# Attention and a two-layer product on one core: norm products on GpSimd, the first batch transposed on TensorE, out matmuls ahead of the scores, w_out in column halves

## The chip, the cores and the metric

The kernel runs on one core of a Trainium2 chip. The metric is the device time of one execution in microseconds (us). Of the timed runs five were classed slow (four of the kernel before in the later series, one of the experiment without the lead); they count in the medians quoted, but in no ratio, and where a slow run moves a difference the text says so. TensorE is called PE in the profile, its weight loads PEld, VectorE DVE, ScalarE ACT, GpSimd POOL and SyncE SP. A line number such as L178 is a line of the kernel that was profiled, so the same statement has different numbers in different kernels.

## The reference

Eight batches, twelve heads, 448 tokens, 64 numbers per head. The result of the attention, heads side by side, goes through a product with w_in (768 x 2048), an activation with a sine, and a product with w_out (2048 x 768).

```python
def rmsnorm(x, g):
    return x / np.sqrt(np.mean(x * x, axis=-1, keepdims=True) + 1e-06) * g
q_n, k_n = rmsnorm(q, g_q), rmsnorm(k, g_k)
scores = np.matmul(q_n, k_n.transpose(0, 1, 3, 2)) / np.sqrt(64)
attn = softmax(scores)                       # over the last axis
x = heads_side_by_side(np.matmul(attn, v))   # (3584, 768)
h = x @ w_in
g = h + np.sin(alpha * h) ** 2 / (alpha + 1e-09)
out = g @ w_out
```

## The kernel before

For each batch there are two stages. An *attention stage* takes six pairs of heads: scores, exponentials, and the product with v. Between them, as "fillers", stand the steps of the out product (w_out) of the batch before, and, as "background", the norm tasks of the batch to come. A *first product stage* is the product with w_in and the sine part ("snake"). Odd batches have 48 filler steps in their attention stage and are called short below; even ones from 2 on have 64 and are called long. A *chunk* is q and k of two pairs of heads; a batch has three chunks. The norm of a chunk, as a list of tasks of which the schedule takes a few per pair:

```python
def square(w): nc.gpsimd.tensor_mul(st[w], qk[ci][:, w], qk[ci][:, w])     # ScalarE for the first chunks
def fold_g():  nc.gpsimd.tensor_mul(qk[ci][:, 1], qk[ci][:, 1], gg)        # VectorE for the first chunks
def reduce(w): nc.vector.reduce_sum(st["ms"][:, w, :], st[w], axis=AX.X)
def rsqrt():   # ScalarE: Ln, then Exp
def scale(w):  nc.vector.tensor_mul(n, x, inv)    # two or three pieces per w, bf16 out
def transpose(): nc.sync.dma_start_transpose(...) # two per chunk
return [lambda: (square(0), square(1)), fold_g, none, lambda: reduce(0), lambda: reduce(1), none,
        rsqrt, lambda: (scale(0), scale(1), transpose())]
```

The schedule of an attention stage (cut):

```python
for p in range(NP):
    scores(pi, 0); scores(pi, 1)
    if p: attend(pi - 1)      # product with v; reciprocal on ScalarE; xT on VectorE
    scores(pi, 3)
    bg(per_slot)
    fill(part[2])             # half of the pair's out steps
    bg(per_slot)
    scores(pi, 2)
    fill(part[3] - part[2])
    bg(per_slot)
    fill(part[4] - part[3])
    bg(per_slot)
...
attend(last pair)
first_product(b)
```

PSUM has four tiles of two banks each for scores, products with v and both products. A tile is free again when its last reader, often VectorE, is done.

The softmax here doesn't subtract the row's maximum and nothing guards it: scores larger than these inputs give would overflow.

## Time and profile before

| | before |
|---|---|
| time, median | 544.5 us |
| span of the profiled run | 543.7 us |
| PE / DVE / ACT / POOL busy | 84% / 54% / 64% / 38% |
| first score matmul | 34.65 us |
| attention stage, short / long | 42.0 / 43.4 us (batches 3 and 4) |
| first product, matmuls | 18.3 us |

The stages in this table run from the end of the matmuls of the first product to the start of the next batch's, so the 3 us of transition belong to the attention stage; the prediction's windows put them into the first product. This is what TensorE waited for in the kernel before, in the view of waits. The columns are the waiting line, what it waited for, us in total, how many times, and the longest:

```profile
PE sc L215 <- DMA qkT<-qkn: 34.6, 1, 34.6
PE ops L305 <- DVE g_sb L258: 11.4, 6, 1.9
PE sc L215 <- DVE xT L244: 10.9, 6, 2.8
```

One wait of 34.6 us for the first transposes, six waits for the last snake piece at the transitions, six for xT in the stages. What the list does not show is the time that matmuls took longer at a lower clock.

### The profile page before, as it was taken

Reading aid. Unit: us, or ns where it says so; the run is one execution under the profiler, and the core shown is the slowest. Engines: PE = TensorE matmul, PEld = TensorE weight load, DVE = VectorE, ACT = ScalarE, POOL = GpSimd, SP = SyncE. Lnnn points to the kernel's source line nnn. Section 1 sums busy time; section 2 is a strip of 40 time slices with the busy share of each in tenths; the row PEclk is TensorE's granted clock in tenths of the full one; section 3 lists DMA queues with packets and bytes.
Section 4 is the critical chain, followed back from the end, with each engine's and each line's share of the span. In section 5 each row is a group of like instructions: output and inputs, shape, how many; then the busy total and the mean of one; then the engine's idle time right before and its main releaser. Section 6 shows DMA issues by size and latency. Waiting matters only on the chain.

```text
span 543.7 us, 7414 instructions
## 1 busy us (share of the span) xinstructions
PE 458.2 (84%) x2816; PEld 214.7 (39%) x2816; DVE 293.5 (54%) x379; ACT 346.0 (64%) x550; POOL 206.2 (38%) x167
## 2 busy tenths in 40 slices
PE   0035589797989999897989999897989999899996
PEld 0011235343444445343444445343444445344553
DVE  0628745368555774377555774377556765222531
ACT  2226377686786657775686657775687658876810
POOL 3004924834257313734258304734257404100400
PEclk9996589799999999898998999898999999999998
DMA  9993599935815565535715564545715551011013
GB/s 226 202 196 76 136 161 210 159 60 125 208 10 72 133 149 113 52 69 128 196 10 72 131 160 103 51 78 119 198 11 70 132 100 27 1 43 45 2 32 85
DMA packets 86276, 56.40 MB, mean 104 GB/s; under 512 B 67552, under 2 KB 81888, under 8 KB 86240
## 3 DMA queue, kind: packets, MB, share of 16 engines
q1 hardware_dynamic: 63344, 42.29, 34.9%
q0 software_dynamic: 21808, 11.80, 17.5%
q10 hardware_dynamic: 1088, 1.84, 1.0%
q8 instruction: 22, 0.36, 0.3%
q14 instruction: 14, 0.11, 0.1%
HBM read 45.69 MB, written 11.01 MB: 104 GB/s over the span
## 4 chain that ended last, share of the span: by engine, by line
PE 63%; DMA 14%; DVE 12%; issue 4%; ACT 3%; POOL 3%; SPq 1%; POOLq 0%; DVEq 0%
PE ops L305 23%; PE hps L269 22%; PE av L238 12%; DMA w_out_sb<-in_moe_w_out_dram 6%; PE sc L215 4%; DVE qkn L180 4%; DMA alpha_sb<-in_moe_alpha_dram 2%; DMA qk<-in_q_dram 2%; DMA qkT<-qkn 2%; DVE qkn L178 2%; DVE g_sb L258 2%; POOL s L253 2%; DVE ms L164 1%; DVE xT L244 1%; PE sc L217 1%
## 5 line engine op out<-in xcount | busy, mean ns | idle before, releaser
L305 PE MATMUL ops<-w_out_sb,g_sb 128*128 128x384 bf16 x896 | 168.9, 339 | 14.3 <-DVE g_sb L258 11.4
L219 ACT ACTIVATE expT<-sc 128x896 bf16<-128x896 f32 x144 | 126.8, 915 | 72.5 <-PE sc L215 72.4
L269 PE MATMUL hps<-xT,w_in_sb 128*128 128x448 bf16 x768 | 146.7, 353 | 0.0
L253 POOL TENSOR_TENSOR s<-s 128x448 f32<-128x448 f32 x64 | 59.8, 934 | 200.4 <-ACT s L250 155.7
L258 DVE SCALAR_TENSOR_TENSOR g_sb<-s,inv_alpha_sb,hps 128x448 bf16<-128x448 f32 x128 | 81.4, 677 | 73.5 <-POOL s L253 73.5
L305 PEld LDWEIGHTS <-g_sb 128*128 128x128 bf16 x896 | 83.6, 100 | 89.8 <-issue 41.7
L157 POOL TENSOR_TENSOR sq<-qk 128x896 f32<-128x896 f32 x42 | 74.3, 1791 | 105.9 <-DMA qk<-in_q_dram 64.6
L269 PEld LDWEIGHTS <-w_in_sb 128*128 128x128 bf16 x768 | 74.5, 98 | 71.5 <-issue 2.9
L215 PE MATMUL sc<-qkT 64*128 64x448 bf16 x288 | 49.2, 382 | 53.4 <-DMA qkT<-qkn 34.6
L250 ACT ACTIVATE s<-hps,alpha_sb 128x448 f32<-128x448 f32 x128 | 73.8, 627 | 30.1 <-PE hps L269 30.1
L238 PE MATMUL av<-expT,vb 128*64 128x448 bf16 (+1 forms) x384 | 75.3, 386 | 9.8 <-ACT expT L219 4.1
L244 DVE TENSOR_TENSOR xT<-av,rec 128x448 bf16<-128x448 f32 x48 | 29.7, 619 | 83.5 <-ACT rec L241 83.5
L238 PE MATMUL av<-expT,ones 128*64 128x448 bf16 (+1 forms) x384 | 73.9, 378 | 0.0
L164 DVE TENSOR_REDUCE ms<-sq 128x14 f32<-128x896 f32 x48 | 51.2, 1076 | 22.5 <-POOL sq L157 22.5
L178 DVE TENSOR_TENSOR qkn<-qk,inv 128x448 bf16<-128x448 f32 x48 | 55.9, 1205 | 6.3 <-ACT inv L169 6.3
L215 PEld LDWEIGHTS <-qkT 64*128 64x128 bf16 x288 | 11.9, 95 | 91.2 <-issue 55.8
L161 POOL TENSOR_TENSOR qk<-qk,gg 128x896 f32<-128x896 f32 x21 | 47.1, 2244 | 1.6
L180 DVE TENSOR_TENSOR qkn<-qk,inv 128x384 bf16<-128x384 f32 x48 | 46.1, 999 | 0.0
L240 ACT ACTIVATE rec<-av 128x448 f32<-128x448 f32 x48 | 26.1, 544 | 31.1 <-PE av L238 31.1
L309 DVE COPY osb<-ops 128x768 f32<-128x768 f32 x28 | 26.7, 954 | 34.1 <-PE ops L305 34.1
L238 PEld LDWEIGHTS <-vb 128*64 128x64 bf16 (+1 forms) x384 | 23.4, 111 | 53.4 <-issue 46.6
L255 ACT ACTIVATE s<-s 128x448 f32<-128x448 f32 x64 | 36.9, 577 | 2.0
(26 smaller groups left out, 179.3 us busy)
## 6 DMA issues: line engine op xcount, KB each, us to landing
out_dram<-osb SPq DMA_DIRECT2D x56, 192.0 KB, 2.7
qk<-in_q_dram SPq DMA_DIRECT2D x22, 448.0 KB, 4.3
qk<-in_k_dram SPq DMA_DIRECT2D x22, 448.0 KB, 4.5
vb<-in_v_dram POOLq DMA_DIRECT2D x16, 288.0 KB, 5.4
w_in_sb<-in_moe_w_in_dram POOLq DMA_DIRECT2D x2, 1536.0 KB, 21.6
w_out_sb<-in_moe_w_out_dram POOLq DMA_DIRECT2D x1, 3072.0 KB, 33.7
qk<-in_q_dram ACTq DMA_DIRECT2D x2, 448.0 KB, 7.3
qk<-in_k_dram ACTq DMA_DIRECT2D x2, 448.0 KB, 8.5
```

The lines of the kernel that those rows point to most:

```text
L157: nc.gpsimd.tensor_mul(st[w], qk[ci][:, w], qk[ci][:, w])
L164: nc.vector.reduce_sum(st["ms"][:, w, :], st[w], axis=AX.X)
L178: nc.vector.tensor_mul(n[:, :, hi, :], x[:, hi], inv[:, hi].unsqueeze(2).to_broadcast([P, NJ, D]))
L180: nc.vector.tensor_mul(n[:, :2 * NT, hi, :].rearrange("p (t jj) d -> p jj t d", jj=2), x[:, hi, :2 * NT].rearrange("p (jj t) d -> p jj t d ...
L215: nc.tensor.matmul(sc[:, hi, :S], kt[r, t * P:(t + 1) * P], qt[r, :], start=True, stop=True)
L219: nc.scalar.activation(expT[pi][:, 2 * t:2 * t + 2, :], sc[:, :, :S], ACT.Exp, scale=SCALE)
L238: nc.tensor.matmul(av[r, bank, :S], lhsT, rhs, start=(t == 0), stop=(t == NT))
L250: nc.scalar.activation(s1, hps, ACT.Sin, scale=alpha_sb[:, m, :])
L253: nc.gpsimd.tensor_mul(s2, s1, s1)
L258: nc.vector.scalar_tensor_tensor(g_sb[:, m, (b % 2) * S:(b % 2 + 1) * S], s2, inv_alpha_sb[:, m, :], hps, op0=ALU.mult, op1=ALU.add)
L269: nc.tensor.matmul(ps[:, m % 2, :S], w_in_sb[:, kt, m * P:(m + 1) * P], x[:, kt, :], start=(kt == 0), stop=(kt == KT - 1))
L305: nc.tensor.matmul(st["ps"][:, half, :HALF], lhsT, w_out_sb[:, m, half * HALF:(half + 1) * HALF], start=(m == 0), stop=(m == MT - 1))
```

## The change

Its intent: VectorE is left with one-input work, GpSimd gets all arithmetic with two SBUF inputs; the first batch need not send its transposes through loaded DMA queues; the time at the start of an attention stage in which the last snake pieces are made is filled with out matmuls; half of w_out is there sooner. The core of the diff, cut:

```diff
-    nc.sync.dma_start(out=gq_sb, ...)          # and gk_sb
+    nc.scalar.dma_start(out=gq_sb, ...)
     def load_w_out():
-        nc.gpsimd.dma_start(out=w_out_sb, in_=...)
+        for half in range(2):
+            nc.gpsimd.dma_start(out=w_out_sb[:, :, cols], in_=src[:, :, cols])
     def scale(w):
+        eng = nc.vector if first else nc.gpsimd        # first: chunk 0
-        nc.vector.tensor_mul(...)
+        eng.tensor_mul(...)
+    def pe_transpose(pp):
+        for w in range(2):
+            for j in range(NJ):
+                nc.tensor.transpose(tp[:, w, j * REST:(j + 1) * REST], st["n"][r, w, j], ident[r, r])
+        nc.vector.tensor_copy(qkT[pi], tp[:, :, :S])
+    if early:                                          # chunks 1 and 2
+        return [sq+fold, none, (reduce(0), reduce(1)), none, (rsqrt, scale(0), scale(1)), none, pe_transpose(0), pe_transpose(1)]
-    return [sq, fold, none, reduce(0), reduce(1), none, rsqrt, (scale(0), scale(1), transpose())]
+    return [sq+fold, none, reduce(0), reduce(1), (rsqrt, scale(0), scale(1)), none, none, transpose]
...
-            for ci in range(NC * (b + 1), NC * (b + 2)):      # next chunk requested with each chunk
+            for ci in range(NC * b + 2, NC * b + 5):          # one chunk later; q and k requested two chunks ahead
...
+            if p == 0:
+                fill(part[2])                 # 8 of the 16 steps of pair 0
             scores(pi, 0)
             scores(pi, 1)
             if p:
                 attend(pi - 1)
+            else:
+                fill(part[3] - part[2])       # 4 more
             scores(pi, 3)
```

Batch 0's out product also goes by column halves of a row tile. Alpha is loaded later, with w_out, and its reciprocal on VectorE stands later too. The smaller changes are not shown: pair 0 takes 16 of the out steps in place of 8 (10 in long stages) and the other pairs take fewer, the norms of a batch spread over the end of one attention stage and the start of the next, and chunk 0 is normalised q first.

## The prediction

> **What bounds the kernel now.** The kernel took 544.6 us (median of 3); the profiled span is 543.7 us. I first read the busy shares: TensorE is busy for 84% of the span, no other engine for more than 64%, so the question is where TensorE idles or runs slowly. I then cut the span at the points where TensorE passes from one stage to the next and asked for busy time per stage. The columns are the stretch, its length, then busy us (and instructions) of PE, weight loads, DVE, ACT and POOL, and the granted clock, DMA share and GB/s:
>
> ```profile
> 0.00:34.60 34.60, 0.00 (x0) 0.00 (x0) 11.12 (x20) 5.84 (x9) 4.64 (x11) 1.00 1.10 204
> 34.60:78.90 44.30, 27.86 (x145) 9.83 (x146) 29.77 (x34) 26.36 (x44) 21.64 (x14) 0.69 0.85 132
> ...
> 202.20:223.60 21.40, 19.16 (x105) 9.69 (x104) 12.16 (x21) 17.25 (x29) 8.87 (x10) 1.00 0.37 83
> 223.60:262.50 38.90, 35.98 (x235) 15.36 (x235) 23.99 (x26) 25.67 (x40) 18.48 (x12) 0.91 0.57 110
> ...
> 406.00:445.20 39.20, 37.89 (x267) 17.95 (x267) 25.45 (x27) 25.35 (x41) 19.04 (x12) 1.00 0.52 96
> ...
> 466.60:499.20 32.60, 32.60 (x235) 14.56 (x235) 6.00 (x8) 23.95 (x35) 0.00 (x0) 1.00 0.10 25
> 499.20:517.40 18.20, 18.20 (x97) 9.41 (x97) 8.71 (x14) 14.22 (x24) 6.54 (x7) 1.00 0.09 23
> ```
>
> Row 1 is a start-up with no matmul at all. Row 2 is the attention of batch 0. Row 3 is a first product with its tail (18.2 us of matmuls, then about 3 us of little). Rows 4 and 6 are the same TensorE work (235 matmuls): with norm arithmetic beside it 38.9 us, without any 32.6 us and no idle. Row 6 and row 7 are therefore what the stages cost when TensorE alone sets the pace. Row 5 is the longer stage (64 out steps, not 48), which needs some 32.6 + 32 x 0.163 = 37.8 us (20.8 us for the 128 out matmuls of the end gives 0.163 each).
>
> The timeline says what TensorE waits for. The start-up, by the normalisation's products and the transpose:
>
> ```profile
> 20.37 1.16 DVE L178 TENSOR_TENSOR qkn<-qk,inv 128x448 bf16<-128x448 f32 x2 [0.64 <-ACT inv L169]
> 21.45 1.02 DVE L180 TENSOR_TENSOR qkn<-qk,inv 128x384 bf16<-128x384 f32 x2
> ...
> 22.70 12.82 SPq L191 DMA_TRANSPOSE qkT<-qkn  x4
> ...
> 34.65 0.93 PE L215 MATMUL sc<-qkT 64*128 64x448 bf16 x4 [34.65 <-DMA qkT<-qkn]
> ```
>
> Chunk 0's scale starts at 20.4; it exists at 22.7, but its DMA transposes land only at 34.6, behind the weight and v loads (204 GB/s in this stretch). Then a middle stage, the stretch 246 to 254; the transition at 223.6; and busy time in one microsecond of it, in the columns of the first view:
>
> ```profile
> 246.03 2.63 DVE L178 TENSOR_TENSOR qkn<-qk,inv 128x448 bf16<-128x448 f32 x2
> ...
> 246.48 3.72 POOL L157 TENSOR_TENSOR sq<-qk 128x896 f32<-128x896 f32 x2 [8.99 <-DMA qk<-in_q_dram]
> ...
> 248.58 4.38 DVE L180 TENSOR_TENSOR qkn<-qk,inv 128x384 bf16<-128x384 f32 x2
> 250.28 2.27 POOL L161 TENSOR_TENSOR qk<-qk,gg 128x896 f32<-128x896 f32 x1
> ...
> 253.75 0.37 PE L215 MATMUL sc<-qkT 64*128 64x448 bf16 x2 [2.81 <-DVE xT L244]
> ```
> ```profile
> 223.57 2.72 PE L305 MATMUL ops<-w_out_sb,g_sb 128*128 128x384 bf16 x8 [1.90 <-DVE g_sb L258]
> ```
> ```profile
> 224.00:225.00 1.00, 1.00 (x5) 0.44 (x3) 0.00 (x0) 1.00 (x2) 1.00 (x3) 0.50 0.96 78
> ```
>
> The two pairs of DVE products that took 1.16 and 1.02 us alone at the start take 2.63 and 4.38 us when GpSimd runs its own squares and folds; xT (L244) stands behind them on the same engine, its PSUM buffer is not released, and TensorE waits 2.81 us. At the transition the first out step waits 1.90 us for the last g_sb, although it needs only m = 0: scores were placed ahead of it. After each such wait the granted clock is 0.50 for some 3 us, so that eight out matmuls take 2.72 us in place of 1.4.
>
> **The Trainium skill.** "SBUF — State Buffer", section "Who interferes with whom": a VectorE instruction with two SBUF inputs contends with a GpSimd instruction that reads SBUF. The trace agrees: 1.31 and 2.19 us for a product that takes 0.58 and 0.51 alone. "GPSIMD Engine Reference", section 3.1: two-input elementwise work costs about 2.6 cycles per element at 1.2 GHz, 2.17 ns. The trace agrees: the fold of 896 elements takes 2.08 us when undisturbed, 2.3 ns each with its fixed part. "TensorE: Matmul & The Clock Gate", Part 1: the array falls to half clock after an idle window of about 3.4 us and returns after about 3.4 us of work. The trace has 0.50 already after a wait of 1.9 us, for about 3 us. The same page, Part 4: a TensorE transpose lands in PSUM and needs a copy afterwards, about 275 to 390 ns for 128x128; no transpose of this kind is in the trace of before.
>
> **The change, part by part.**
>
> *Start-up.* q lands at 5.3 (the gate copy) and k by 7.6. ScalarE's table load ends at 7.0; square q 0.94, reduction of q 1.08, Ln and Exp 0.55 bring the q scale to about 9.9; two products 1.16 (to 11.0), reduction of k 1.08 (12.1), fold 1.03 (13.2), scale of k 1.30 (14.5). The second half of the TensorE transposes (seven of 64 columns, my estimate 0.1 us each at half clock) ends at 15.3, the copy of 896 PSUM columns is about 1 us (the 768-wide copy takes 0.95): first scores near 16.3 in place of 34.6. gq and gk now lead their queue; they landed at 11.1 before and bound nothing so long as they land before about 9. Gain 18.3 us.
>
> *First batch.* Little is gained here. ScalarE needs 6 x 4.4 us for exponentials and reciprocals (3 x 0.92 + 0.53 + 0.54 + 0.58 per pair), plus 3.6 for squares and about 2.2 for the roots: 32 us. TensorE at half clock needs 6 x 2.83 x 2 = 34 us (2.83 is 32.6 less 96 x 0.163, over six pairs), plus 56 transposes at 0.1, some 5. The transposes of chunk 2 stand on TensorE only three slots behind their scale, which GpSimd takes 4.7 us for: about 4 us of waiting. GpSimd must then do fold, scale and squares of chunks 3 and 4 and issue v and w_out (about 5 us of issuing) before reductions and roots that stand ahead of exponentials. I take 41 us for 44.3: gain 3.3. The first product begins near 57.5 in place of 78.9.
>
> *GpSimd's new load.* From 0.93 us for 448 and 1.68 for 896 elements (squares) the fixed part is 0.19; with the fold's 2.08, a scale costs 0.19 + 2.11 ns per element: 1.13 for 448 (x2), 1.0 for 384 (x2), 0.46 for 128, so 4.7 us per chunk. Squares 3.37 and fold 2.08 make it 10.2 us per chunk, three chunks 30.5, plus 3 us to issue v: 33.5 us in an attention stage of 32.6 or 37.8, plus 7.5 us (8 x 0.93) in the first product. Per batch 41 of 51 or 56 us. It holds, but in the short stages with little to spare. DVE loses 110 us of products (55.9 + 46.1 + 8.6) less 2.5 for chunk 0, and with them every collision of two-SBUF-input work.
>
> *Short attention stages (b = 1, 3, 5).* From 41.6 (with the 3.0 us wait for w_out), 38.9 and 39.0 towards 32.6. I leave 2.5 us for GpSimd's lag: each chunk takes about 10.5 us with its gaps and its two pairs of heads take 2 x 4.9, and behind the v issue it begins about 3 us late, so the last reduction makes ScalarE and xT late by 1 to 2 us once, with some half clock. 35.1 each: gains 6.5, 3.8, 3.9. *Long ones (b = 2, 4, 6):* 40.8, 40.4, 39.2 to 38.6: gains 2.2, 1.8, 0.6. *b = 7* now carries chunk 23: minus 0.5.
>
> *Transitions.* Eight out steps (16 matmuls, 2.6 us) with m = 0 to 7 now fill the time in which the last sines, squares and g_sb (3.1 us) are done. Each 21.4 us becomes 18.5: six times 2.9 is 17.4. The first product of batch 0 goes from 19.5 to 18.3: 1.2.
>
> *w_out in halves.* It landed 33.7 us after its issue. Issued near 40, behind v, the first half is there near 62 and the second near 78; the first is needed at about 76, the second some 17 us later. Nothing waits, at 96 weight loads more that lie under matmuls (100 ns under 163).
>
> Sum: 18.3 + 3.3 + 1.2 + 6.5 + 3.8 + 3.9 + 2.2 + 1.8 + 0.6 - 0.5 + 17.4 = 58.5 us; 544.6 - 58.5 = 486.
>
> **The rivals.** (1) GpSimd becomes the bound: its three- and four-dimensional patterns with a bf16 output are not in the trace, and at 7 us per chunk for the scale the short stages need 3 x 12.5 + 3 = 40 us, and the first batch 5 more: about 505. For it: reductions on DVE and roots on ScalarE wait in order for GpSimd. Against: the other two-input forms cost 1.7 to 2.3 ns per element, and nothing is left to collide. (2) The early start is eaten in batch 0, where weights still load, TensorE waits in order for GpSimd's scale, and the clock is at half: with 49 us there, about 494. For it: the 0.69 clock of row 2 and the short distance from scale to transpose. (3) TensorE sets the pace everywhere after batch 0: 7.5 and 3 us of my allowances fall away, and batch 0 takes its 35 us: about 470. For it: row 6, which has no idle at all. (4) The norms' move does nothing because the DVE was not the cause; then only start-up and transitions gain, some 37 us: about 507. Against it: the 2.81 us wait stands right behind the stretched products.
>
> **Range and chances.** Most errors I can name lengthen: 472 to 503 holds the time 8 times in 10. Start-up and transitions alone are 36 us, 6.6%, and rest on waits that are seen, so faster by over 2% has 0.97, within 2% 0.02, slower 0.01.
>
> **What would show it.** Right: first score matmul at 15 to 19 us; no wait of TensorE for g_sb between first product and out steps, and a clock near 1.00 there; short stages of 33 to 36 us; GpSimd busy about 310 us (206 plus 23 scales of 4.7), DVE about 190; no wait for w_out. Wrong: scale products well over 1.1 us on GpSimd, TensorE waiting for the transposes' input by more than 5 us in batch 0, reductions waiting for squares by more than a few us per stage, or a first batch longer than 44 us.

## The result, and the profile after

The changed kernel took 488.85 us (median of 4, 487.6 to 489.0), the kernel before 544.54 in the same series. The ratio is 0.898 (95% interval 0.894 to 0.902). Ratios here are the mean time of one kernel's fast runs over the mean of the other's fast runs of the same rounds, so not quite the ratio of the medians. The prediction was 486 us, 472 to 503: right, by 3 us. Its terms were less right than its sum.

The changed kernel's stages, in the columns of the prediction's first view: start-up, attention of batch 0, first product of batch 0, attention of batch 1, a short stage (batch 3), a long one (batch 6):

```profile
0.00:16.00 16.00, 1.68 (x28) 1.36 (x28) 6.45 (x13) 5.79 (x9) 6.21 (x14) 1.00 0.91 201
16.00:62.30 46.30, 28.60 (x201) 11.58 (x202) 14.13 (x18) 26.46 (x44) 32.92 (x33) 0.85 1.28 206
62.30:82.00 19.70, 19.70 (x97) 9.83 (x98) 8.91 (x15) 14.22 (x24) 7.66 (x9) 0.93 0.67 121
82.00:117.60 35.60, 33.83 (x242) 14.91 (x240) 14.83 (x21) 28.02 (x44) 30.02 (x28) 1.00 0.69 151
...
192.60:225.90 33.30, 33.30 (x242) 14.57 (x240) 14.39 (x18) 27.99 (x44) 29.98 (x27) 1.00 0.67 128
...
352.60:391.10 38.50, 38.50 (x273) 17.70 (x272) 14.84 (x19) 28.14 (x44) 31.00 (x29) 1.00 0.54 97
```

In the last two rows PE is busy for the whole stretch at full clock. From batch 2 to the end of the last product TensorE alone sets the time. Stage by stage, from the first score matmul and the start and end of each first product:

| stage | before | after | difference |
|---|---|---|---|
| to the first score matmul | 34.65 | 16.04 | -18.6 |
| attention of batch 0 | 44.2 | 46.2 | +1.9 |
| first product of batch 0 | 18.3 | 19.8 | +1.5 |
| attention of batch 1 | 42.75 | 35.5 | -7.3 |
| short, batches 3 and 5 | 42.0, 42.05 | 33.25, 33.25 | -17.6 |
| long, batches 2, 4, 6 | 43.85, 43.4, 42.2 | 38.45 each | -14.1 |
| attention of batch 7 | 35.6 | 33.25 | -2.4 |
| first products 1 to 7 | 18.33 each | 18.33 each | 0 |
| out product of batch 7 and last store | 26.2 | 26.3 | 0 |

The differences add up to -56.5, which is the difference of the spans (543.7 to 487.2). The start, from the timeline (start, us, engine, line, operation, matmuls merged, and in brackets the idle time before and its releaser):

```profile
11.65 0.55 PE L212 MATMUL tp<-ident,qkn 64*128 64x64 bf16 x7 [11.65 <-DVE qkn L189]
14.78 1.13 PE L212 MATMUL tp<-ident,qkn 64*128 64x64 bf16 x21 [2.58 <-DVE qkn L191]
16.04 0.93 PE L239 MATMUL sc<-qkT 64*128 64x448 bf16 x4
```

The transposes follow the scale products at once and the scores follow the transposes; no DMA stands between. The norm of chunk 0 itself ends 7.8 us sooner, at 14.9 in place of 22.7: in the kernel before VectorE stood idle for 5.22 us, until 16.54, ahead of the reciprocal of alpha, which waited for alpha's DMA with the rest of the norm behind it. The prediction did not name that wait. At a transition, where the kernel before waited 1.90 us for g_sb, the same view has the out matmuls run on from the first product, with the scores behind them:

```profile
135.68 2.76 PE L330 MATMUL ops<-w_out_sb,g_sb 128*128 128x384 bf16 x16
138.37 0.55 PE L239 MATMUL sc<-qkT 64*128 64x448 bf16 x4
```

In GpSimd's timeline, the scale products of one chunk, which were VectorE's 2.63 and 4.38 us in the stretch that the prediction showed:

```profile
93.74 1.84 POOL L189 TENSOR_TENSOR qkn<-qk,inv 128x448 bf16<-128x448 f32 x2 [1.69 <-ACT inv L179]
95.53 1.62 POOL L191 TENSOR_TENSOR qkn<-qk,inv 128x384 bf16<-128x384 f32 x2
97.11 0.41 POOL L196 TENSOR_TENSOR qkn<-qk,inv 128x128 bf16<-128x128 f32 x1
```

They take 3.9 us per chunk, and nothing stretches them. What TensorE still waits for, in the view of waits, is nearly all in batch 0:

```profile
PE av L262 <- ACT expT L243: 3.9, 1, 3.9
PE tp L212 <- POOL qkn L189: 3.6, 1, 3.6
PE av L262 <- DMA vb<-in_v_dram: 3.5, 2, 1.8
...
PE ops L330 <- DVE g_sb L282: 0.5, 2, 0.3
```

### The profile page after: what moved, and what is told of

The parts are those of the page before. It is cut to its first block, busy times and chain, and to the rows that moved or that the text cites. A ratio compares the mean times of both kernels' runs of the same rounds, so it can differ in the third digit from the quotient of the medians.

```text
span 487.2 us, 7555 instructions
## 1 busy us (share of the span) xinstructions
PE 447.9 (92%) x2900; PEld 213.0 (44%) x2900; DVE 194.9 (40%) x271; ACT 343.5 (71%) x552; POOL 290.9 (60%) x287
## 3 DMA queue, kind: packets, MB, share of 16 engines
q1 hardware_dynamic: 57968, 40.85, 36.3%
q0 software_dynamic: 23872, 11.80, 19.8%
## 4 chain that ended last, share of the span: by engine, by line
PE 82%; POOL 7%; DMA 5%; ACT 2%; DVE 1%; issue 1%; POOLq 0%
PE hps L293 30%; PE ops L330 29%; PE av L262 15%; PE sc L239 6%; DMA vb<-in_v_dram 3%; POOL sq L167 2%; PE sc L241 2%; DMA qk<-in_q_dram 1%; POOL qkn L191 1%; POOL vb L104 1%; POOL qk L171 1%; POOL qkn L189 1%; DMA qkT<-qkn 1%; POOL vb L109 1%; DVE ms L174 1%
## 5 line engine op out<-in xcount | busy, mean ns | idle before, releaser
L330 PE MATMUL ops<-w_out_sb,g_sb 128*128 128x384 bf16 x896 | 161.9, 327 | 0.5 <-DVE g_sb L282 0.5
L330 PEld LDWEIGHTS <-g_sb 128*128 128x128 bf16 x896 | 80.8, 98 | 72.0 <-issue 23.5
L262 PE MATMUL av<-expT,ones 128*64 128x448 bf16 (+1 forms) x384 | 71.8, 368 | 0.0
L167 POOL TENSOR_TENSOR sq<-qk 128x896 f32<-128x896 f32 x42 | 70.1, 1698 | 0.0
L189 POOL TENSOR_TENSOR qkn<-qk,inv 128x448 bf16<-128x448 f32 x46 | 42.2, 939 | 39.7 <-ACT inv L179 35.2
L239 PE MATMUL sc<-qkT 64*128 64x448 bf16 x288 | 46.3, 371 | 6.2 <-ACT expT L243 3.3
L264 ACT ACTIVATE rec<-av 128x448 f32<-128x448 f32 x48 | 26.1, 544 | 33.3 <-PE av L262 33.2
L262 PEld LDWEIGHTS <-vb 128*64 128x64 bf16 (+1 forms) x384 | 22.4, 111 | 53.0 <-issue 43.9
L335 DVE COPY osb<-ops 128x768 f32<-128x768 f32 (+1 forms) x31 | 27.2, 877 | 32.6 <-PE ops L330 30.3
L191 POOL TENSOR_TENSOR qkn<-qk,inv 128x384 bf16<-128x384 f32 x46 | 37.2, 831 | 0.0
L265 ACT ACTIVATE rec<-rec 128x448 f32<-128x448 f32 x48 | 27.7, 576 | 1.5
```

The costliest lines, as they stand in the source:

```text
L189: eng.tensor_mul(n[:, :, hi, :], x[:, hi], inv[:, hi].unsqueeze(2).to_broadcast([P, NJ, D]))
L239: nc.tensor.matmul(sc[:, hi, :S], kt[r, t * P:(t + 1) * P], qt[r, :], start=True, stop=True)
L262: nc.tensor.matmul(av[r, bank, :S], lhsT, rhs, start=(t == 0), stop=(t == NT))
L330: nc.tensor.matmul(st["ps"][:, k, :HALF], lhsT, w_out_sb[:, m, half * HALF:(half + 1) * HALF], start=(m == 0), stop=(m == MT - 1))
```

## The experiments

Twelve kernels ran in three series, all correct. Each series has its own runs of the kernel before (medians 543.7, 543.3 and 541.7 us), against which the ratios are taken. The change itself did not run in them, so differences to it go from one series to another; a run that equals it in work (q and k one chunk ahead) took 488.56 us in the second. My theory after the result: the start is worth 18 us and is gained whole; the lead is worth 2 to 3 us at each of seven transitions; the rest of the middle stages came from ending VectorE's collisions with GpSimd. The rivals stand with each run.

| run | median us | ratio to before |
|---|---|---|
| the change | 488.85 | 0.898 (0.894 to 0.902) |
| scale on VectorE | 501.46 | 0.922 (0.920 to 0.925) |
| no lead | 508.86 | 0.934 (0.930 to 0.937) |
| first batch by DMA | 511.77 | 0.941 (0.938 to 0.945) |
| one more square per chunk on GpSimd | 498.44 | 0.917 (0.915 to 0.919) |
| scale on VectorE, at the chunk's end | 499.72 | 0.919 (0.914 to 0.925) |
| q and k one chunk ahead | 488.56 | 0.897 (0.891 to 0.904) |
| the lead alone, on the kernel before | 523.78 | 0.964 (0.957 to 0.970) |
| w_out in one transfer | 484.47 | 0.891 (0.886 to 0.897) |
| and early issue | 484.41 | 0.895 (0.891 to 0.900) |
| w_out in one transfer, w_in behind v | 487.40 | 0.901 (0.897 to 0.905) |
| early issue and w_in behind v | 487.46 | 0.900 (0.895 to 0.904) |
| early issue, chunk 2 transposed later | 480.45 | 0.888 (0.884 to 0.892) |

**Scale products on VectorE.**

```diff
-            eng = nc.vector if first else nc.gpsimd
+            eng = nc.vector
```

> The changed kernel with the scale products of every chunk put back on VectorE, everything else as changed. Theory (the middle stages gained because VectorE no longer has work with two SBUF inputs that blocks and is blocked by GpSimd): the scale products take 1.0 to 2.5 us in place of 0.58 and 0.51 where GpSimd squares or folds beside them, TensorE waits again behind xT, attention stages b = 1 to 6 grow by 2 to 5 us each, 500 to 510 us in all. Rival (the middle stages gained from the new order of norm tasks and the earlier q and k loads; which engine scales is indifferent): 485 to 491 us.

Measured 501.46 us, 12.6 more than the change. The middle stages fall short of the theory: short ones take 35.55 us (+2.3), long ones do not change at all (38.45). Half of the loss is in batch 0, whose attention takes 52.6 us in place of 46.2. The timelines of VectorE and TensorE there:

```profile
33.59 4.47 DVE L189 TENSOR_TENSOR qkn<-qk,inv 128x448 bf16<-128x448 f32 x2 [0.27 <-ACT inv L179]
```
```profile
38.12 0.55 PE L212 MATMUL tp<-ident,qkn 64*128 64x64 bf16 x7 [6.16 <-DVE qkn L189]
```

Two products of 0.58 us each take 4.47 beside GpSimd's issue of w_out and its squares, and TensorE, which takes its transposes in order, waits 6.16 us. So collisions are real, but in the middle stages the engine alone, with the lead in place, explains only 2.3 of the 8.8 us that a short stage gained, and nothing of a long one's gain. What the engine is worth without the lead was not run.

**Without the lead.**

```diff
             if p == 0:
-                fill(part[2])
...
+            fill(part[2]); bg(1); scores(pi, 2); fill(part[3] - part[2])   # as in the kernel before
```

> The changed kernel without out matmuls ahead of the scores at pair 0 (the same 16 steps stay in pair 0, behind the scores as before). Theory (the lead fills the 3 us in which the last snake pieces are made): each of the seven transitions loses about 3 us to waiting and half clock, 505 to 512 us. Rival (the time is hidden, since the exponentials queue behind the snake anyway and TensorE catches up later in the stage): 488 to 493 us.

Measured 508.86, 20.0 more than the change (19.2 without its slow run): the theory holds. A short stage takes 35.6 us, a long one 40.8 (batch 4), 2.35 more each; batches 1, 2 and 7 lose 3.2 to 4.0. At the transition the wait is that of the kernel before, to 0.01 us, but in this stage the matmuls behind it run at full speed. The timeline, then the busy time in two microseconds from 203.8, with the clock third from the right:

```profile
202.86 2.76 PE L330 MATMUL ops<-w_out_sb,g_sb 128*128 128x384 bf16 x16 [1.89 <-DVE g_sb L282]
```
```profile
203.80:205.80 2.00, 2.00 (x14) 0.98 (x11) 0.00 (x0) 1.24 (x2) 2.00 (x2) 1.00 1.43 164
```

Sixteen matmuls in 2.76 us, where eight took 2.72 in the kernel before after a wait of 1.90. A wait of 1.9 us may or may not cost the clock. The traces show on what this hangs. In each of the fourteen traces the stretches of half clock, but for the last one of the trace, last 3.41 us or a multiple of it, and they start a multiple of 3.413 us apart (in the kernel before at 161.98 and 223.42, for example, 18 times 3.413): the clock changes on a fixed grid, whose step is 3.413 us. The busy time in the step that holds the transition's wait, in batch 3 of the kernel before, then in batches 2 and 3 of this run:

```profile
220.01:223.42 3.41, 1.32 (x9) 0.43 (x8) 2.41 (x4) 2.86 (x4) 2.15 (x3) 1.00 0.00 0
```
```profile
139.72:143.13 3.41, 1.42 (x9) 0.84 (x9) 1.31 (x3) 3.35 (x5) 3.33 (x5) 1.00 0.20 12
201.16:204.57 3.41, 1.71 (x11) 1.06 (x11) 1.27 (x2) 3.38 (x5) 3.41 (x6) 1.00 0.43 37
```

TensorE (first number after the comma) was busy for 1.32 and 1.42 of 3.41 us in the first two, and half clock followed at 223.42 and 143.13; in the third it was busy for 1.71 us, as part of the wait fell into the step before, and full clock followed. In the fourteen traces no stretch of half clock begins after a step that was busy for half or more. After less than half one mostly does, but not always (full clock followed 1.52 us in batch 5 of this run and 1.69 in batch 6 of the kernel before). So it is the place of the wait on the grid that decides here. (The start is left out of this: up to 31.1 us the changed kernel's clock is given as 1.00, but a pair of matmuls takes about 0.6 us, as it does later at half clock, and not the 0.35 to 0.38 of full clock.) Batches 1, 2 and 7 of this run, the ones that lose 3.2 to 4.0, have such a stretch, the others have none; in the kernel before four of the six waits for g_sb are followed by one.

**The first batch transposed by DMA.**

```diff
-                    ..., none, lambda: pe_transpose(0), lambda: pe_transpose(1)]
+                    ..., none, none, transpose]        # and likewise for chunk 0
```

> The changed kernel with DMA transposes in place of TensorE transposes for chunks 0 to 2. Theory (the loaded DMA queues make the transpose late): chunk 0 is normalised near 15 us, the transposes take 8 to 12 us, first scores near 25 us, and 495 to 501 us in all. Rival (batch 0 is bounded anyway by v, which lands at 25.4 us, and by GpSimd's chain later): first scores near 25 us too, but only 488 to 493 us.

Measured 511.77, 22.9 more than the change; both theory and rival were too small. The queue of SyncE and TensorE's first scores, from the timelines:

```profile
15.09 17.86 SPq L202 DMA_TRANSPOSE qkT<-qkn  x2
```
```profile
37.54 0.93 PE L239 MATMUL sc<-qkT 64*128 64x448 bf16 x4 [37.54 <-DMA qkT<-qkn]
```

Chunk 0 is normalised near 15 us, nearly 8 us sooner than in the kernel before, and its scores start 3 us later than there. The transposes took up to 22.4 us to land, against a median of 3.7 us over the whole kernel. So the early norm is worth nothing without the TensorE transposes: on top of it these are worth 21.5 us to the first scores. What they are worth without the early norm was not run. Attention of batch 0 then takes 44.9 us in place of 46.2, so the waiting for v at 20.8 and 25.4 us, which is gone here, hides little of it.

**One more square per chunk on GpSimd.**

```diff
                 nc.gpsimd.tensor_mul(st[w], qk[ci][:, w], qk[ci][:, w])
+                if w == 0:
+                    nc.gpsimd.tensor_mul(st[w], qk[ci][:, w], qk[ci][:, w])
```

> The changed kernel with one more square (1.7 us, into the same place) on GpSimd in each of the chunks 3 to 23. Theory (GpSimd, busy 30 us of the 33.3 us of a short stage, is close to the bound): short stages b = 1, 3, 5 grow to 35 to 37 us each, batch 0 by 3 us (two such chunks), long stages stay at 38.5: 497 to 503 us. Rival (in-order waiting has slack enough everywhere): 488 to 492 us.

Measured 498.44: the theory holds for the stages. Short stages take 35.05 us (+1.8) and long ones are unchanged at 38.45; batch 0 grows by 1.2 us, not by 3, and batch 1 goes to 39.5, with a wait of 3.35 us and a stretch of half clock behind it, which the theory did not have. The short stage of batch 3:

```profile
198.00:233.10 35.10, 33.86 (x242) 15.12 (x240) 14.02 (x18) 28.10 (x44) 33.81 (x29) 1.00 0.64 122
```

GpSimd is busy 33.8 of 35.1 us. With 30.0 of 33.3 the changed kernel is within one square per chunk of being bound by GpSimd in its short stages.

**Scale on VectorE, at the end of the chunk.** The first two runs leave 4.1 us of a short stage's 8.8 unexplained. My next theory was the place of the products in the chunk.

```diff
-                lambda: (rsqrt(slice(0, 2)), scale(0), scale(1)), none, none, transpose]
+                lambda: rsqrt(slice(0, 2)), lambda: (scale(0), scale(1), transpose())]
```

> The scale products on VectorE, and in chunks 3 to 23 also at the end of the chunk's eight tasks, just ahead of the next chunk's squares and fold, where the kernel before had them (loads still two chunks ahead). Theory (of the 8.8 us that a short stage lost, 2.4 were the lead and 2.3 the engine; the other 4.1 come from the place of the products: at the end of a chunk they meet the next chunk's GpSimd work, in the middle they mostly meet an idle GpSimd): short stages near 39.5 us instead of 35.6, long ones 40 to 41 instead of 38.5, 510 to 518 us in all. Rival (the 4.1 us come from the loads two chunks ahead): short stages stay near 35.6 us and the kernel near 501 us.

Measured 499.72. Short stages take 36.1 us, 0.55 more than with the products in the middle, long ones 38.6. The theory falls: the place of the products is not it. (The early batches trade places, which was not followed up: batch 0 takes 43.35 us in place of the 52.6 of scale on VectorE, batch 1 44.1 in place of 37.1, with a wait of 4.5 us.)

**q and k one chunk ahead.**

```diff
-        if ci + 2 < NC * B:
-            tasks[0] = lambda t=tasks[0]: (t(), load_qk(ci + 2))
+        if 2 <= ci < NC * B - 1:
+            tasks[0] = lambda t=tasks[0]: (t(), load_qk(ci + 1))
```

> The changed kernel with each chunk's q and k requested one chunk ahead, not two. Theory (place of the products, see the run with the late VectorE scale): no or little change, 488 to 492 us, since the loads of 4 to 5 us have one and a half pairs of heads to land. Rival (GpSimd idled up to 9 us for q in the kernel before, so the early loads are what keeps it in time): GpSimd waits for q by more than 2 us per chunk, short stages 35 to 38 us, 495 to 505 us.

Measured 488.56, the same as the change; every stage agrees within 0.3 us. The earlier loads do nothing here: GpSimd waits for no load in the middle stages with either. Whether its waits of up to 9.7 us for q cost the kernel before anything is not shown, as that kernel did not run with earlier loads.

**The lead alone, on the kernel before.**

```diff
+            if p == 0: fill(part[2])
             scores(pi, 0); scores(pi, 1)
-            if p: attend(pi - 1)
+            if p: attend(pi - 1)
+            else: fill(part[3] - part[2])
```

> The kernel before with nothing but the lead of out matmuls at pair 0 (eight steps ahead of the scores, four behind the second scores). Theory: seven transitions at 2.4 to 4 us each, as taking the lead from the changed kernel cost 20 us; 524 to 530 us, though batch 1 has to wait for w_out as before. Rival (in the kernel before, VectorE's stretched products give the gain back later in the stage): 537 to 543 us.

Measured 523.78, 19.5 less than the kernel before, 0.2 us under the theory's range. It also bears on the missing 4.1 us. The short stage of batch 3 in four kernels:

| | no lead | lead |
|---|---|---|
| norm as before (scale on VectorE) | 42.0 | 36.3 |
| norm as changed (scale on GpSimd) | 35.6 | 33.25 |

The rows differ in more than the engine: the order of the tasks and the loads go with it, and of the 3.1 us between the rows with the lead the engine is 2.3 (35.55 us with scale on VectorE). Without the lead, the upper kernel gives pair 0 eight out steps and the lower one sixteen. In this stage either step alone saves about 6 us; the second to be added saves 2.4 to 3.1. The busy times of that stage in the kernel before, with the lead alone, and without the lead:

```profile
220.50:262.50 42.00, 36.84 (x241) 15.70 (x240) 26.00 (x30) 28.70 (x44) 20.80 (x14) 0.92 0.53 101
```
```profile
213.30:249.70 36.40, 33.74 (x242) 14.93 (x240) 24.82 (x30) 28.45 (x44) 20.83 (x14) 1.00 0.61 114
```
```profile
199.80:235.40 35.60, 33.37 (x241) 14.84 (x240) 14.43 (x18) 27.98 (x44) 29.93 (x27) 1.00 0.63 120
```

The idle time adds up: length less PE busy is 5.2 us in the first row, 2.7 in the second, 2.2 in the third (and 0 in the changed kernel). What does not add up is the clock. Only the first row has one below 1.00, and there the same matmuls are busy 36.8 us in place of 33.3. Those 3.5 us are all but 0.6 of the missing part. They are two stretches of half clock, of 3.41 us each: one from 223.42, behind the wait for g_sb, and one from 254.14, behind the wait of 2.81 us for xT that the prediction showed. With the lead, the first wait is gone and the wait for xT is 0.94 us. Without the lead, the wait for g_sb is as long as before and only falls elsewhere on the grid.

So the table is not a rule of its own: that curing one fault also cures the clock is in part the luck of this stage. In the long stage of batch 6 the kernel before has no half clock (42.2 us); the lead alone takes 42.2 there, with a stretch from 414.96, the changed kernel without the lead 40.8, both steps 38.45. Each of these kernels left one profile, so how often a stretch falls into a stage from run to run is not known.

**w_out in one transfer.**

```diff
-        for half in range(2):
-            nc.gpsimd.dma_start(out=w_out_sb[:, :, cols], in_=src[:, :, cols])
+        nc.gpsimd.dma_start(out=w_out_sb, in_=src)
-        units = ... if b else [(i, (h,)) for h in range(2) for i in range(NT)]
+        units = [(i, (0, 1)) for i in range(NT + odd)]
```

> The changed kernel with w_out in one transfer and batch 0's out product by whole rows. Theory (both halves landed before 72 us, the first out matmul runs at 82 us): no change, 487 to 491 us, batch 1's attention 35 to 36 us. Rival (the halves are what keeps batch 1 from waiting): a wait of 2 us or more for w_out and 491 to 496 us.

Measured 484.47, about 4 us less than the change (488.56 for the run beside it that equals the change). Neither theory nor rival said so: the halves cost. They landed 18.7 and 29.5 us after their issues at 40.8 and 42.0, so by 71.5 at the latest, and were first needed at 81.8. Two costs show. One is in batch 1, 33.25 us in place of 35.5; all five runs that keep w_out whole have 33.25 there. By halves, the first unit reaches m = 14 and 15 after 2.4 us, before the last snake pieces are there (0.24 and 0.26 us of waiting), and there are six copies out of PSUM in place of three, one of which TensorE waited for behind VectorE's reductions:

```profile
111.03 0.38 PE L262 MATMUL av<-expT,vb 128*64 128x448 bf16 x2 [0.87 <-DVE osb L335]
```

The other is in batch 0: 42.6 us in place of 46.2, though its only edit there is one GpSimd issue less (1.22 us against 2.37). Chunk 3's squares begin 1.3 us sooner, so do its reductions and the roots, behind which ScalarE has the next exponentials. ScalarE's wait for them, in the timeline of the change and of this run:

```profile
47.70 0.32 ACT L178 ACTIVATE inv<-ms,eps 128x28 f32<-128x28 f32 x1 [2.95 <-DVE ms L174]
```
```profile
46.40 0.32 ACT L176 ACTIVATE inv<-ms,eps 128x28 f32<-128x28 f32 x1 [1.61 <-DVE ms L172]
```

TensorE waits 1.49 us there in place of 2.83, and its clock from 43 us to the end of the stage is 1.00 in place of 0.81. With the shorter wait there is no half clock before the first product, and 1.3 us become 3.6. That is one profile of each; the grid of the run without the lead applies here too.

**v of batch 1, alpha and w_out issued after pair 0** (on top of the single transfer).

```diff
-            if b == 0 and p == 2:
+            if b == 0 and p == 0:
                 load_alpha(); load_v(1); load_w_out()
```

> The version with w_out in one transfer, and with v of batch 1, alpha and w_out issued at the end of batch 0's pair 0 in place of pair 2. Theory (in batch 0 GpSimd's chain of scale, 4 us of issuing, squares, then reductions and roots ahead of exponentials sets the pace; taking one issue of 1.2 us out of it by the single transfer brought 3.6 us): batch 0's attention falls from 42.6 to 37 to 40 us, the kernel to 479 to 482 us. Rival (the DMA queues are the limit of batch 0, 206 GB/s; the earlier w_out delays q, k or w_in): 484 us or more.

Measured 484.41 and 42.0 us of attention in batch 0: no gain. Chunk 3's squares begin at 37.6 in place of 41.9, but the roots and exponentials behind them are at most 0.6 us sooner, and GpSimd waits 3.4 us for the roots of chunk 3. The chain of issues had been the limit only up to the 1.3 us that the single transfer removed. The rival's number holds, but not its reason: nothing waits for q, k or w_in.

**w_in behind v** (on top of the single transfer).

```diff
     load_v(0)
+    nc.gpsimd.tensor_copy(vgate, vb[0][:, 0:2, 0])     # and one for the last piece of v
     load_w_in()
```

> The version with w_out in one transfer, and with w_in issued only when v of batch 0 has landed. Theory (v, waited for at 20.8 and 25 us, shares its engines with w_in): v lands some microseconds sooner, the two waits of about 3 us go, the kernel 481 to 484 us. Rival (one queue is served in order, v has preference over w_in already and is late by the q and k loads): v lands as before, 484 to 486 us.

Measured 487.40: a miss, by 3 us the other way. v does land sooner, at 20.7 in place of 25, as the theory had it, but the gate stands on GpSimd, in order:

```profile
20.72 0.18 POOL L355 COPY vgate<-vb 128x2 bf16<-128x2 bf16 x1 [0.34 <-DMA vb<-in_v_dram]
21.18 1.32 POOL L140 DMA_DIRECT2D w_in_sb<-in_moe_w_in_dram  x2 [0.27 <-issue]
22.50 2.10 POOL L169 TENSOR_TENSOR qk<-qk,gg 128x896 f32<-128x896 f32 x1
```

The fold of chunk 1 begins at 22.5 in place of 14.9, and TensorE waits 2.5 and 1.2 us for that chunk's scale. One wait was traded for another; batch 0's attention takes 45.6 us.

**Both together.**

> The two changes of batch 0 together: v of batch 1, alpha and w_out issued at the end of pair 0, and w_in behind v of batch 0. If both theories hold and add up, 476 to 480 us; if w_in then becomes late for the first product, a wait for it shows there and the kernel loses again.

Measured 487.46, batch 0's attention 48.3 us: a miss too. The gate's cost is larger here: v's last piece lands at 22.9 and GpSimd's early issues stand ahead of chunk 2's fold. No wait for w_in shows.

**Chunk 2's transposes later** (on the early issue).

```diff
-                    ..., scale(1)), none, lambda: pe_transpose(0), lambda: pe_transpose(1)]
+                    ..., scale(1)), none] + [none, none] * (ci == 2) + [lambda: pe_transpose(0), lambda: pe_transpose(1)]
-            bg(1 if b else 2)
+            bg(1 if b else 4 if p == 3 else 2)
```

> The early issue, and chunk 2's TensorE transposes two task slots later (with two more tasks in pair 3's first slot). Theory (TensorE waits 3.6 and 1.0 us for GpSimd's scale of chunk 2 because the transposes stand three slots behind it): the waits of 4.6 us shrink to about 1, the kernel 2 to 4 us below the early issue alone. Rival (exponentials are the limit of batch 0, ScalarE only waits elsewhere): within 1 us of the early issue.

Measured 480.45, 4.0 under the early issue: the theory holds. The waits for chunk 2's scale shrink from 4.6 to 1.1 us and batch 0's attention to 38.4. This version beats both kernels: 0.888 of the kernel before, 8.4 us under the change (from another series). What it still waits for is at the end of batch 0, where the roots of chunk 4 stand ahead of the last exponential. Their squares on GpSimd had waited 0.8 and 1.5 us for q and k:

```profile
53.01 0.58 PE L260 MATMUL av<-expT,vb 128*64 128x448 bf16 x2 [3.70 <-ACT expT L241]
```

## Why the prediction was right or wrong

- **Start-up: right.** 16.04 us against 16.3, gain 18.6 against 18.3. The DMA run shows that nothing of it is left without TensorE's transposes; how the gain divides between them and the earlier norm is open.
- **First batch: the wrong size.** 41 us were allowed and 46.2 measured, half way and more to the second rival's 49; a first batch longer than 44 us was one of the prediction's own signs of being wrong. The step that failed is the sum of waits: the 4 us for chunk 2's transposes were there (3.57 and 1.02), but v's landing (1.8 and 1.65 us) was not thought of, the roots ahead of exponentials cost waits of 2.8 and 3.9 us, and the latter left the first product to begin at half clock, 19.8 us in place of 18.3. The work of the transposes was no part of the loss: 28 of them took 1.46 us, some 0.05 each, where 0.1 was estimated.
- **GpSimd's new load: the mechanism right, the size too high.** A chunk's scale takes 3.9 us, not 4.7. The prediction took its cost per element from the fold (2.11 ns); the squares that it read beside it give (1.68 - 0.93) / 448 = 1.67, and with that and its fixed 0.19 us come out at the measured 0.94, 0.83 and 0.41. GpSimd is busy 290.9 us, not 310 (206 plus 23 times 4.7 is 314): 23 chunks of 0.8 are 19 of it, and the squares, 1.70 us each in place of 1.79, another 4. The first rival (7 us per scale) is out. That it holds with little to spare is right: 1.7 us more per chunk lengthen the short stages.
- **Middle stages: too high by the lag.** 2.5 us were left for GpSimd's lag in short stages, and 0.8 in long ones. In batches 2 to 7 it costs nothing, as the third rival said of that part. Part of this is the scale's real length. Batch 1 came out at 35.5, near its term of 35.1, but for a reason that was not in the term: the halves of w_out.
- **Why the middle stages gained: half right.** The fourth rival (the norms' move does nothing) is out, since either half of the two-by-two table shows a gain. But VectorE's collisions are only a part: scale on VectorE costs the changed kernel 2.3 us per short stage and nothing in the long ones. The idle times of the two faults add up; the clock does not. The prediction read half clock after each such wait; in its own trace it follows four of the six waits for g_sb. Whether it follows depends on where the wait falls on the grid of 3.41 us, so no single stage gives a cure its share of the clock.
- **Transitions: right.** 2.9 us each were expected; taking the lead away costs 2.35 to 4.0 per stage, 20.0 in all (19.2 from fast runs), and waits for g_sb fell from 11.4 to 0.5 us. On the kernel before the lead saves 19.5 in all, but in the profiles from nothing (batch 6) to 5.7 us in a stage.
- **w_out in halves: wrong in sign.** "Nothing waits" for the data, as said, but the term counted 96 more weight loads, which there are not (896 for the out product in both kernels), and forgot the second issue on GpSimd and the doubled copies out of PSUM. It was worth about +4 us, not 0.

The sum hit 486 against 488.85 because 6.7 us too little in batch 0 stood against some 5 us too much in batches 2 to 6. That is luck. What is not settled: where, below half of a step of the grid, the clock starts to fall (both were seen between 1.5 and 1.7 us of busy time), and what part the engine of the scale products has in the kernel without the lead.

## What to carry to other kernels

Where one engine sets the pace at a clock that falls with idleness, the costs of two waits are not a sum: look for the clock beside the wait, and look at every stage of a kind before giving a cure its share, for the same wait costs the clock in one stage and not in the next. In a start-up and a first batch, count the instructions that stand ahead on each in-order engine, DMA issues among them; a DMA split in two for earlier landing is paid for in issue and, if the work is split with it, in copies out of PSUM, and is worth it only if somebody waited for the data. A transpose that the first work hangs on does not belong on queues which the weights fill.

## What the Trainium skill lacked or had wrong

- "TensorE: Matmul & The Clock Gate", Part 1, has the clock halve after an idle window of about 3.4 us, and says that the window runs freely. The grid of 3.41 us is in every trace here. But the windows before half clock were not idle: TensorE was busy for 1.32 and 1.42 us of two of them, and 1.71 us kept full clock. The page does not say how little is enough.
- "GPSIMD Engine Reference", section 3.1, gives about 2.6 cycles per element for two inputs. As the whole time over the count the scale products agree: 448 elements took 939 ns and 384 took 831, 2.5 and 2.6 cycles each at the page's 1.2 GHz. As the cost of one element more the figure is too high: between these two sizes it is 1.69 ns, 2.0 cycles, and some 0.2 us is fixed, for which the section has no number.
- No page gives the time from issue to landing of a DMA transpose in loaded queues: in the run with the first batch by DMA, 3.7 us to landing as a median, and up to 22.4 us beside the loads of the weights.
